# Attention and a two-layer network in one kernel: the first v split ahead of w_out, the last w_out blocks later in the load order, the second scores in one PSUM bank

## The chip, the cores and the metric

The kernel runs on one core of a Trainium2 chip. Measured is the device time of one execution in microseconds; the profile is of one such execution. TensorE (PE, with its weight loads PEld) multiplies, VectorE (DVE) and ScalarE (ACT) work on vectors, SyncE's queue (SP) issues the DMAs. Each engine takes its instructions in the order of the program.

## The reference, cut to what matters

```python
# q, k, v: (2, 6016, 256);  w_in: (256, 2048);  w_out: (2048, 256);  alpha: (2048,)
qn = q / (norm(q, axis=1) + 1e-6)          # norm over the 6016 rows
kn = k / (norm(k, axis=1) + 1e-6)
s  = kn.transpose(0, 2, 1) @ qn / tau      # (2, 256, 256)
a  = softmax(s, axis=-1)                   # sum + 1e-9
x  = (v @ a).reshape(12032, 256)
h  = x @ w_in
g  = maximum(h, 0) + alpha * minimum(h, 0)
out = g @ w_out                            # (12032, 256)
```

## The kernel before, in words

The order of all work is written out by hand (`tc.manual_schedule()`): an engine runs its instructions in the order in which the program names them, and the framework only adds the waits that the data and the buffers ask for.

**Scores.** q and k of a batch come in 25 chunks, `load_kq`, of two blocks of 128 rows (the first and the last two chunks of one). `chunk_pe` (L357) multiplies a chunk into two 128x256 sums S of the batch, 8 matmuls for a chunk of two blocks; `chunk_elem` takes the squares of batch 0. S0 is summed first. Its norms, scores, exponentials and transposes follow, while TensorE goes on with the first chunks of S1 (batch 1). Before, S1 lies in the two banks `o0` and `o1`, which stage two of the items uses afterwards.

**M.** `x @ w_in` is folded: for each of 8 pairs of blocks (NPAIR) of w_in, `m_pe` (L482) multiplies the softmax with w_in, `m_sums` (L493) makes sums of its quarters on ScalarE and VectorE and `m_split` (L510) splits them into a rounded high part and a low part (`split`, L93 to L98). The loop of L708 does this for j = 0 to 7, with a chunk or two of S1 on TensorE beside each.

**Weights.** w_in and w_out come as 64-bit numbers in 8 blocks each. `conv_a` (L218, ScalarE, L189 to L191) and `conv_b` (L227, VectorE, L195 to L202) convert block c: c = 0 to 7 are w_in's, 8 to 15 w_out's. `split_wo` (L242) then splits a w_out block into high (ScalarE, L248) and low (VectorE, L249). In the loop of L708 pass j converts block j + 3 (ScalarE) and j + 2 (VectorE), so w_out's blocks 0 to 2 are begun in it. After the loop the kernel before runs the S1 chunks up to number 19 and splits w_out blocks 0 to 7 in order; the first v split stands behind `split_wo(5)`, and behind ScalarE's conversion of block 7.

**v.** v comes transposed in 24 tiles of 504 or 500 columns, 12 a batch. `v_sums` (VectorE, L287), `v_high` (ScalarE, L306) and `v_low` (VectorE, L312) make seven combinations of a tile's quarters and split them. The raw tile has one buffer, the split tiles have two (`vspl`); each pair of conversions took one of these as scratch.

**Items.** The main loop (L807) goes over 192 items, tile by tile, 8 pairs each. An item's first stage multiplies M with v in seven products of three matmuls (`pe_a` to `pe_d`; L102 to L104). ScalarE copies the first into two banks (`copies`, L543, L544), VectorE adds one product over (`add_p7`, L560, once with n = 0 after `pe_b`, once with n = 1 after `pe_c`), ScalarE and VectorE apply the function (`act_n`, L572; `dve_g`, L581) and split the result (`g_high`, L590; `g_low`, L594). Stage two (`stage2`, L599; L618) runs three items later: 12 matmuls with w_out in two parts of 5 and 7. `pe_c` of an item needs its L560 of n = 0; `pe_d` writes what the L560 of n = 1 reads and waits for it. In items 0 to 2, which have no stage two, six places are filled with the last chunks of S1 (FILL = 5 of them), and `evac` (L368, two VectorE copies, L371) takes S1 out behind the last. `at_item(i, f)` puts side work behind item i's own: the split of the next v tile, batch 1's norms and M.

Four "set" matmuls (L744) stand ahead of item 0; they write the four banks of the first stage once, with the first v split as moving operand.

**Loads.** The list `mix` gives the order of the loads behind S0's: i a w_in block, k an S1 chunk (two DMAs), o a w_out block, v the first v tile. Each kind has its ring of buffers: `raw`, 4 buffers, for i, o and later the transposed q and k; `m`, `gh` and `gl` for the chunks. A load is put in SP's queue at the point of the program where its buffer has come free, and never past another that still waits; in the queue it waits for the last reader of that buffer. The load of the next v tile is issued where `v_low(t, 0)` stands.

Of the kernel before, what the change touches and what calls it, by code (L numbers as in the profile page):

```python
# [8 lines left out]
F32 = mybir.dt.float32  # L9
F32R = mybir.dt.float32r  # L10
U32 = mybir.dt.uint32
# [3 lines left out]
P = 128  # L15
TW = 512
# [1 line left out]
LATE = 3  # L18
TL = 1024
WARM = 8  # L20
FILL = 5


@with_exitstack
def fused_kernel(
# [28 lines left out]
    B, N, C = q.shape  # L54
    DFF = w_in.shape[1]
    DM = w_out.shape[1]
    KC = C // P
# [3 lines left out]
    NPAIR = NF // 2  # L61
# [28 lines left out]
    def f32(ap):  # L90
        return ap.bitcast(F32)
# [15 lines left out]
    class Loads:  # L107


        def __init__(self, rings):  # L110
            self.free = dict(rings)
            self.todo = []
# [39 lines left out]
    big = {}  # L152
# [21 lines left out]
    def convert_a(w, src, c):  # L174

        if c % 2 == 0:
            big["cv"] = vpool.tile([P, 2, 3, 512], U32, tag="vspl", name=f"cv{c}")
        s = big["cv"][:, c % 2]
        d, a, l = s[:, 0], s[:, 1], f32(s[:, 2])
        if w is None:
            w = l
        nc.scalar.activation(f32(d), f32(src[:, :, 1]), AF.Copy, scale=2.0**-112)  # L189
        nc.scalar.activation(l, src[:, :, 0], AF.Copy, scale=2.0**-29, bias=2.0**23)  # L190
        nc.scalar.activation(l.bitcast(U32), l, AF.Copy, bias=-(2.0**23))  # L191
        return d, a, l, w
# [25 lines left out]
    def conv_a(c):  # L218

        if c < NPAIR:  # L220
            src, w = wi_raw.pop(c).rearrange("p k f t -> p (k f) t"), wi[:, c].rearrange("p k f -> p (k f)")
        else:
            src, w = wo_raw.pop(c - NPAIR).rearrange("p f m t -> p (f m) t"), None
        half[c] = convert_a(w, src, c)
        loads.done("raw")

    def conv_b(c):  # L227
        w = convert_b(nc.vector, *half.pop(c))
        if c >= NPAIR:
            wo32[c - NPAIR] = w  # L230
# [11 lines left out]
    def split_wo(i):  # L242

        w = wo32.pop(i).rearrange("p (f m) -> p f m", f=2)
        for fi in range(2):
            f = 2 * i + fi
            s = sgn[:, f : f + 1]
            nc.scalar.activation(wo[:, 0, f], w[:, fi], AF.Copy, scale=s)  # L248
            nc.vector.scalar_tensor_tensor(  # L249
                out=wo[:, 1, f], in0=w[:, fi], scalar=s, in1=f32(wo[:, 0, f]),  # L250
                op0=ALU.mult, op1=ALU.subtract,
            )
# [24 lines left out]
    def v_sums(t, part):  # L277
        h = tiles[t][2] // 2
        x = v_raw[t]
        if part == 0:  # L280
            v_tmp[t] = vtpool.tile([P, 4, HW_], F32, tag="vt", name=f"vt{t}")
        s = v_tmp[t]
        b11, b12 = x[:, 0, :h], x[:, 0, h : 2 * h]
        b21, b22 = x[:, 1, :h], x[:, 1, h : 2 * h]
        sums = ((1, b12, b11), (3, b22, b12), (2, b22, s[:, 1, :h]), (0, b21, s[:, 2, :h]))
        for o, i0, i1 in sums[2 * part : 2 * part + 2]:
            nc.vector.tensor_tensor(out=s[:, o, :h], in0=i0, in1=i1, op=ALU.subtract)  # L287
# [13 lines left out]
    def v_high(t, part):  # L301
        h = tiles[t][2] // 2
        if part == 0:
            v_spl[t] = vpool.tile([P, 2, 7, HW_], F32R, tag="vspl", name=f"vs{t}")
        for sl, x in v_parts(t, part):
            nc.scalar.copy(v_spl[t][:, 0, sl, :h], x)  # L306
# [27 lines left out]


    class Attn:
        def __init__(self, b, S):
            self.b = b
            self.S = S
            self.sums = sm.tile([P, KC], F32, tag="sums", name=f"sums{b}")  # L340
# [16 lines left out]
        def chunk_pe(self, ci):  # L357
            n = chunks[ci][1]
            t = kq_raw.pop((self.b, ci))
            for j in range(n):  # L360
                for cc in range(KC):
                    nc.tensor.matmul(  # L362
                        self.S[cc], t[:, 0, j, cc * P : cc * P + P], t[:, 1, j, :],
                        start=ci == 0 and j == 0, stop=ci == NCH - 1 and j == n - 1,
                    )
            loads.done(kq_ring(self.b, ci))

# [142 lines left out]
    def m_split(at, j):  # L510
        b = at.b
        m = mpool.tile([P, 2, 7, P], F32R, tag="m", name=f"m{b}_{j}")
        split(m[:, 0], m[:, 1], mx.pop((b, j))[:, 0:7], nc.scalar)
        M[b, j] = m
# [116 lines left out]
    with tc.manual_schedule():  # L631
# [18 lines left out]
        for ci in range(NCH):  # L650
            loads.add(kq_ring(0, ci), lambda ci=ci: load_kq(0, ci))
            if ci == 4:
                loads.add("small", load_small)
        mix = "iikikikkikikikikkkkokkokvkokkokkkookkkkoko"
        count = dict.fromkeys("ikov", 0)
        for x in mix:
            j = count[x]
# [24 lines left out]
                a0.chunk_pe(ci - LATE)  # L682
        np_ = ps_r.tile([P, TW], F32, tag="r1", name="np0")
        pb = ps_r.tile([P, TW], F32, tag="r1", name="pb0")
        pt = [ps_q.tile([P, TW], F32, tag="q", name="pt0"), ps_a.tile([P, TW], F32, tag="at", name="pt1")]
        po = [ps_o.tile([P, TW], F32, tag=f"o{cc}", name=f"S1_{cc}") for cc in range(KC)]
        a1 = Attn(1, [x[:, 0:C] for x in po])
        conv_a(0)
        a0.chunk_pe(NCH - 3)
        conv_b(0)  # L690
# [15 lines left out]
        a0.split_eT(1)  # L706
        nxt = 3
        for j in range(NPAIR):  # L708
            conv_a(j + 3)
            conv_b(j + 2)  # L710
            if j < 2:
                a1.chunk_pe(nxt)
                nxt += 1
            m_pe(a0, j, ps_r, f"r{j % 2}")
            a1.chunk_pe(nxt)
            nxt += 1
            m_sums(a0, j)
            if j:
                m_split(a0, j - 1)
        m_split(a0, NPAIR - 1)  # L720
        while nxt < NCH - FILL:
            a1.chunk_pe(nxt)
            nxt += 1
        split_wo(0)
        conv_a(NPAIR + 3)
        for i in range(2, NPAIR):
            conv_b(NPAIR + i)
            split_wo(i - 1)
            if i + 2 < NPAIR:
                conv_a(NPAIR + i + 2)  # L730
            if i == NPAIR - 2:
                for part in range(2):
                    v_sums(0, part)
                for part in range(3):
                    v_high(0, part)
                for part in range(3):
                    v_low(0, part)
        split_wo(NPAIR - 1)

        h = max(w for _, _, w in tiles) // 2  # L740
        assert h == tiles[0][2] // 2
        for f in (0, 1, 0, 1):
            x = ps_r.tile([P, 2, HW_], F32, tag=f"r{f}", name="set")
            nc.tensor.matmul(  # L744
                x[:, :, :h], wo[:, 0, 0, 0:P], v_spl[0][:, 0, 0:2, :h], start=True, stop=True,
                skip_group_check=True,
            )

# [3 lines left out]
        def at_item(i, f, *args):  # L752
            side.setdefault(i, []).append((f, args))


        i = NPAIR + 4
        for p in range(len(pieces)):
# [24 lines left out]
            at_item(i, lambda j=j: (m_pe(a1, j, ps_a, "at"), m_sums(a1, j)))  # L782
            at_item(i + 1, lambda j=j: m_split(a1, j))
        for t in range(1, len(tiles)):
            i = (t - 1) * NPAIR + 1
            at_item(i, v_sums, t, 0)
            at_item(i + 1, v_sums, t, 1)
            at_item(i + 1, v_high, t, 0)
            at_item(i + 2, v_high, t, 1)
            at_item(i + 2, v_low, t, 0)  # L790
            at_item(i + 3, v_high, t, 2)
            at_item(i + 3, v_low, t, 1)
            at_item(i + 4, v_low, t, 2)

        fill = iter(range(NCH - FILL, NCH))

# [73 lines left out]
```

## Time and profile before

| | |
|---|---|
| median of 3 runs | 1137.34 us (1136.93 to 1138.18) |
| profiled execution | 1138.28 us, its span 1136.4 us |
| TensorE busy | 1118.8 us, 98% of the span |
| VectorE busy | 840.9 us, 74% |
| ScalarE busy | 810.7 us, 71% |
| DMA | 71.14 MB, most of it in the first tenth of the span |

Times of single instructions are microseconds from the span's start. In a timeline a row is a run of like instructions: its start, the time from the first start to the last end, the engine, the line, the operation, what it writes and reads, how many, and in brackets the engine's idle time before it with what ended it. Instructions of one engine overlap a little when they follow each other without a wait, so the distance from start to start is shorter than the duration; the ends of matmuls are modelled.

### The profile page before, as it was taken

What the parts mean: (1) busy time and instruction counts of PE and PEld (TensorE: products, weight loads), DVE (VectorE), ACT (ScalarE), POOL (GpSimd) and SP (SyncE); (2) the same over time, 40 slices, a digit from 0 to 9 for tenths busy, and PEclk for the clock granted to TensorE, in tenths of its full rate; (3) what the DMA queues carried; (4) which work ended last, traced back from release to release, by engine and by line L of the source; (5) the groups of instructions that cost most, each with busy time, mean ns of one, the idle gap of its engine ahead of it and who ended that gap; (6) DMA issues with size and microseconds to landing.
All of it is one profiled execution on the core that took longest, in us unless ns stands there. A gap on an engine that the chain in (4) does not pass through costs nothing.

```text
span 1136.4 us, 17786 instructions
## 1 busy us (share of the span) xinstructions
PE 1118.8 (98%) x6884; PEld 1008.8 (89%) x6884; DVE 840.9 (74%) x1562; ACT 810.7 (71%) x1498; POOL 1.7 (0%) x8
## 2 busy tenths in 40 slices
PE   9996999999999999999999999999999999999998
PEld 8885899889999999899999989999999999999997
DVE  6787777777777777877777877777777777777765
ACT  6786677877877776776776766766776776776764
POOL 0000000000000000000000000000000000000000
PEclk9997999999999999999999999999999999999999
DMA  9997002222222110110100101100100100110000
GB/s 338 346 320 272 20 19 59 88 72 75 74 73 73 53 37 1 37 36 2 37 21 17 38 1 37 38 10 28 37 19 19 37 19 19 37 31 8 19 20 18
DMA packets 36019, 71.14 MB, mean 63 GB/s; under 512 B 3680, under 2 KB 17504, under 8 KB 35936
## 3 DMA queue, kind: packets, MB, share of 16 engines
q1 hardware_dynamic: 35936, 70.01, 18.5%
q8 instruction: 54, 0.88, 0.3%
q14 instruction: 29, 0.24, 0.1%
HBM read 57.68 MB, written 12.32 MB: 62 GB/s over the span
## 4 chain that ended last, share of the span: by engine, by line
PE 93%; DVE 3%; DMA 2%; ACT 1%; issue 0%; SPq 0%; POOL 0%; DVEq 0%; ACTq 0%; POOLq 0%
PE o L618 46%; PE r L102 10%; PE r L104 10%; PE r L103 10%; PE S L362 4%; PE q L103 4%; PE q L104 4%; PE q L102 4%; PE pm L491 1%; DMA wo<-w_out_dram 1%; DMA kq<-q_dram 1%; DVE m L98 0%; DMA kq<-k_dram 0%; PE warm L639 0%; DVE cv L199 0%
## 5 line engine op out<-in xcount | busy, mean ns | idle before, releaser
L618 PE MATMUL o<-gh,wo 128*128 128x500 f32 (+1 forms) x1536 | 508.7, 392 | 1.4 <-ACT ob L622 1.4
L581 DVE SCALAR_TENSOR_TENSOR g<-r,sgn,g 128x500 f32<-128x500 f32 (+1 forms) x384 | 282.3, 735 | 106.6 <-ACT g L572 106.6
L618 PEld LDWEIGHTS o<-gh,wo 128*128 128x128 f32 x1536 | 276.4, 188 | 41.3 <-ACT ob L622 1.6
L618 PE MATMUL o<-gl,wo 128*128 128x500 f32 (+1 forms) x768 | 299.3, 390 | 0.0
L572 ACT ACTIVATE g<-r,salpha 128x500 f32<-128x500 f32 (+1 forms) x384 | 262.8, 688 | 22.2 <-PE r L104 1.5
L560 DVE TENSOR_TENSOR r<-r,p 128x250 f32<-128x250 f32 (+1 forms) x384 | 163.7, 426 | 145.0 <-PE r L104 145.0
L102 PE MATMUL r<-vs,m 128*128 128x250 f32 (+1 forms) x960 | 269.1, 280 | 1.0 <-DVE r L560 0.8
L104 PE MATMUL r<-vs,m 128*128 128x250 f32 (+1 forms) x960 | 268.1, 279 | 0.0
L103 PE MATMUL r<-vs,m 128*128 128x250 f32 (+1 forms) x960 | 267.8, 279 | 0.0
L590 ACT CAST gh<-g 128x500 fp32r<-128x500 f32 (+1 forms) x384 | 230.0, 613 | 48.9 <-DVE g L581 45.8
L543 ACT COPY r<-q 128x500 f32<-128x500 f32 (+1 forms) x192 | 108.3, 564 | 201.6 <-PE q L104 201.6
L594 DVE TENSOR_TENSOR gl<-g,gh 128x500 fp32r<-128x500 f32 (+1 forms) x384 | 242.5, 673 | 4.7 <-ACT gh L590 4.7
L102 PEld LDWEIGHTS r<-vs,m 128*128 128x128 f32 x960 | 180.9, 188 | 17.6 <-DVE r L560 1.0
L103 PEld LDWEIGHTS r<-vs,m 128*128 128x128 f32 x960 | 181.5, 189 | 15.3
L104 PEld LDWEIGHTS r<-vs,m 128*128 128x128 f32 x960 | 181.4, 189 | 0.0
L618 PEld LDWEIGHTS o<-gl,wo 128*128 128x128 f32 x768 | 144.1, 188 | 23.6
L103 PE MATMUL q<-vs,m 128*128 128x250 f32 (+1 forms) x384 | 107.5, 280 | 0.4 <-DVE vs L312 0.4
L104 PE MATMUL q<-vs,m 128*128 128x250 f32 (+1 forms) x384 | 107.6, 280 | 0.0
L102 PE MATMUL q<-vs,m 128*128 128x250 f32 (+1 forms) x384 | 107.4, 280 | 0.0
L362 PE MATMUL S<-kq 128*128 128x256 f32 x332 | 76.0, 385 | 0.0
L103 PEld LDWEIGHTS q<-vs,m 128*128 128x128 f32 x384 | 72.6, 189 | 0.7 <-DVE vs L312 0.7
L102 PEld LDWEIGHTS q<-vs,m 128*128 128x128 f32 x384 | 72.6, 189 | 0.3 <-ACT vs L306 0.3
(82 smaller groups left out, 716.2 us busy)
## 6 DMA issues: line engine op xcount, KB each, us to landing
kqT<-kqT_dram SPq DMA_DIRECT2D x20, 512.0 KB, 3.6
kq<-k_dram SPq DMA_DIRECT2D x39, 256.0 KB, 5.5
kq<-q_dram SPq DMA_DIRECT2D x39, 256.0 KB, 5.6
v<-vT_dram SPq DMA_DIRECT2D x16, 500.0 KB, 3.6
outT_dram<-ob SPq DMA_DIRECT2D x32, 250.0 KB, 2.0
wi<-w_in_dram SPq DMA_DIRECT2D x8, 512.0 KB, 5.5
wo<-w_out_dram SPq DMA_DIRECT2D x8, 512.0 KB, 5.7
v<-vT_dram SPq DMA_DIRECT2D x8, 504.0 KB, 3.6
```

Source lines behind the costliest of these rows:

```text
L102: nc.tensor.matmul(out, wh, xh, start=first, stop=False, **s)
L103: nc.tensor.matmul(out, wh, xl, start=False, stop=False, **s)
L104: nc.tensor.matmul(out, wl, xh, start=False, stop=last, **s)
L362: nc.tensor.matmul(self.S[cc], t[:, 0, j, cc * P : cc * P + P], t[:, 1, j, :], start=ci == 0 and j == 0, stop=ci == NCH - 1 and j == n - 1,)
L491: nc.tensor.matmul(o, at.eT[:, d, cs], wi[:, j, d, :], start=first, stop=last)
L543: nc.scalar.copy(r_t[i][0][:, :, :h], x[:, 0:1, :h].broadcast_to([P, 2, h]))
L560: nc.vector.tensor_tensor(out=r[1][:, n, :h], in0=r[0][:, 1, :h], in1=p7_t[i][:, :h], op=ALU.add)
L572: nc.scalar.activation(by_half(g_t[i][:, fi], i), r_t[i][fi][:, :, : half_of(i)], AF.Copy, scale=salpha[:, f : f + 1],)
L581: nc.vector.scalar_tensor_tensor(out=g, in0=r_t[i][fi][:, :, : half_of(i)], scalar=sgn[:, f : f + 1], in1=g, op0=ALU.mult, op1=ALU.max,)
L590: nc.scalar.copy(gs_t[i][0][:, fi, :w], g_t[i][:, fi, :w])
L594: nc.vector.tensor_tensor(out=gs_t[i][1][:, fi, :w], in0=g_t[i][:, fi, :w], in1=f32(gs_t[i][0][:, fi, :w]), op=ALU.subtract,)
L618: nc.tensor.matmul(o, x, y, start=first, stop=last)
```

## The change

- The scratch of the conversions becomes one tile of 7 parts, used in turn; a w_in block uses 2 (its third is the block itself), a w_out block 3. It takes one of the two `vspl` buffers, so the first v split has the other.
- In the load order the first v tile and w_out blocks 0 to 5 come earlier, each block between single S1 chunks; blocks 6 and 7 come behind chunks 18 and 24.
- S1's two sums share the bank `at`; only the first of the two clears it. The second tile of batch 0's transposes goes to `r1`.
- `split_wo(0)` goes into the last pass of the M loop, ahead of `conv_a(10)`; the whole first v split follows the loop at once. `wo_next(i)` (split block i, ScalarE's part of block i + 2, VectorE's of i + 1) runs for 1 and 2 behind it and, as side work, for 3 to 7 in items 0 to 4.
- FILL goes from 5 to 6: chunk 19 becomes the first fill.
- The set matmuls take a block of M in place of one of w_out as weights.
- The v split of tile 1 runs in items 4 to 7 in place of 1 to 5.

```diff
-FILL = 5
+CV = 7
+FILL = 6
...
-        if c % 2 == 0:
-            big["cv"] = vpool.tile([P, 2, 3, 512], U32, tag="vspl", name=f"cv{c}")
-        s = big["cv"][:, c % 2]
-        d, a, l = s[:, 0], s[:, 1], f32(s[:, 2])
+        if c == 0:
+            big["cv"] = vpool.tile([P, CV, 512], U32, tag="vspl", name="cv")
+            big["at"] = 0
+
+        def part():
+            i = big["at"]
+            big["at"] = (i + 1) % CV
+            return big["cv"][:, i]
+
+        d, l = part(), f32(part())
         if w is None:
-            w = l
+            a, w = part(), l
+        else:
+            a = w.bitcast(U32)
...
-                        start=ci == 0 and j == 0, stop=ci == NCH - 1 and j == n - 1,
+                        start=ci == 0 and j == 0 and not (self.shared and cc),
+                        stop=ci == NCH - 1 and j == n - 1, skip_group_check=self.shared,
...
-        mix = "iikikikkikikikikkkkokkokvkokkokkkookkkkoko"
+        mix = "iikikikkikikikik" + "ko" * 2 + "v" + "ko" * 4 + "k" * 5 + "o" + "k" * 6 + "o"
...
-        pt = [ps_q.tile([P, TW], F32, tag="q", name="pt0"), ps_a.tile([P, TW], F32, tag="at", name="pt1")]
-        po = [ps_o.tile([P, TW], F32, tag=f"o{cc}", name=f"S1_{cc}") for cc in range(KC)]
-        a1 = Attn(1, [x[:, 0:C] for x in po])
+        pt = [ps_q.tile([P, TW], F32, tag="q", name="pt0"), ps_r.tile([P, TW], F32, tag="r1", name="pt1")]
+        po = ps_a.tile([P, KC, C], F32, tag="at", name="S1")
+        a1 = Attn(1, [po[:, cc] for cc in range(KC)], shared=True)
...
         for j in range(NPAIR):
+            if j == NPAIR - 1:
+                split_wo(0)
             conv_a(j + 3)
             conv_b(j + 2)
...
         m_split(a0, NPAIR - 1)
+        for part in range(2):
+            v_sums(0, part)
+        for part in range(3):
+            v_high(0, part)
+        for part in range(3):
+            v_low(0, part)
+
+        def wo_next(i):
+
+            split_wo(i)
+            if i + 2 < NPAIR:
+                conv_a(NPAIR + i + 2)
+            if i + 1 < NPAIR:
+                conv_b(NPAIR + i + 1)
+
+        for i in (1, 2):
+            wo_next(i)
         while nxt < NCH - FILL:
             a1.chunk_pe(nxt)
             nxt += 1
-        split_wo(0)
-        conv_a(NPAIR + 3)
-        for i in range(2, NPAIR):
-            conv_b(NPAIR + i)
-            split_wo(i - 1)
-            if i + 2 < NPAIR:
-                conv_a(NPAIR + i + 2)
-            if i == NPAIR - 2:
-                for part in range(2):
-                    v_sums(0, part)
-                for part in range(3):
-                    v_high(0, part)
-                for part in range(3):
-                    v_low(0, part)
-        split_wo(NPAIR - 1)
...
-                x[:, :, :h], wo[:, 0, 0, 0:P], v_spl[0][:, 0, 0:2, :h], start=True, stop=True,
+                x[:, :, :h], M[0, 0][:, 0, 0], v_spl[0][:, 0, 0:2, :h], start=True, stop=True,
...
+        for i in range(3, NPAIR):
+            at_item(i - 3, wo_next, i)
...
-            i = (t - 1) * NPAIR + 1
-            at_item(i, v_sums, t, 0)
-            at_item(i + 1, v_sums, t, 1)
-            at_item(i + 1, v_high, t, 0)
-            at_item(i + 2, v_high, t, 1)
-            at_item(i + 2, v_low, t, 0)
-            at_item(i + 3, v_high, t, 2)
-            at_item(i + 3, v_low, t, 1)
-            at_item(i + 4, v_low, t, 2)
+
+            when = (1, 2, 2, 3, 3, 4, 4, 5) if t > 1 else (4, 4, 5, 5, 6, 6, 7, 7)
+            steps = (
+                (v_sums, 0), (v_sums, 1), (v_high, 0), (v_high, 1),
+                (v_low, 0), (v_high, 2), (v_low, 1), (v_low, 2),
+            )
+            for i, (f, part) in zip(when, steps):
+                at_item((t - 1) * NPAIR + i, f, t, part)
```

## Rows read from the trace of the kernel before

**Rows 1.** The page: part 1, and S's line of part 5 (busy, mean ns).

```profile
PE 1118.8 (98%) x6884; PEld 1008.8 (89%) x6884; DVE 840.9 (74%) x1562; ACT 810.7 (71%) x1498; POOL 1.7 (0%) x8
...
L362 PE MATMUL S<-kq 128*128 128x256 f32 x332 | 76.0, 385 | 0.0
```

**Rows 2.** The list of waits: engine, what, line <- releaser: us, times, longest.

```profile
PE set L744 <- ACT vs L306: 10.0, 1, 10.0
```

**Rows 3.** Timeline of all engines, 78 to 118 us.

```profile
81.61 13.98 PE L362 MATMUL S<-kq 128*128 128x256 f32 x64
...
104.56 0.92 ACT L306 CAST vs<-v 128x252 fp32r<-128x252 f32 x2 [0.56 <-DVE wo L249]
...
105.53 2.05 PE L744 MATMUL set<-vs,wo 128*128 128x504 f32 x4 [9.95 <-ACT vs L306]
...
112.42 0.47 PE L102 MATMUL r<-vs,m 128*128 128x252 f32 x1
```

**Rows 4.** Windows of 10 us: length, busy by engine (instructions), PEclk, DMA share, GB/s.

```profile
100.00:110.00 10.00, 4.12 (x12) 3.21 (x13) 8.76 (x19) 6.90 (x15) 0.00 (x0) 0.50 0.71 243
...
120.00:130.00 10.00, 9.20 (x63) 8.38 (x62) 9.68 (x21) 8.28 (x16) 0.00 (x0) 1.00 0.01 2
```

**Rows 5.** Chain of waits in order of time: start, us, what.

```profile
133.43 1.61 PE o L618 x7
...
138.64 1.61 PE o L618 x7
```

**Rows 6.** Timeline, VectorE at the M loop's end.

```profile
80.48 1.02 DVE L507 TENSOR_TENSOR mx<-mx 128x128 f32<-128x128 f32 x4
...
81.41 1.09 DVE L98 TENSOR_TENSOR m<-mx,m 128x896 fp32r<-128x896 f32 x1
```

**Rows 7.** Timeline, w_out blocks on ScalarE, then on VectorE.

```profile
92.71 0.89 ACT L248 ACTIVATE wo<-cv,sgn 128x256 fp32r<-128x256 f32 x2
...
93.51 0.66 ACT L189 ACTIVATE cv<-wo 128x512 f32<-128x512 f32 x1
...
95.31 0.89 ACT L248 ACTIVATE wo<-cv,sgn 128x256 fp32r<-128x256 f32 x2
...
94.03 0.42 DVE L195 TENSOR_SCALAR cv<-cv 128x512 uint32<-128x512 uint32 x1
...
95.84 0.88 DVE L249 SCALAR_TENSOR_TENSOR wo<-cv,sgn,wo 128x256 fp32r<-128x256 f32 x2
```

**Rows 8.** Timeline, VectorE in items 1 and 2, and TensorE's wait.

```profile
119.41 0.43 DVE L560 TENSOR_TENSOR r<-r,p 128x252 f32<-128x252 f32 x1 [0.57 <-PE r L104]
...
119.75 0.73 DVE L581 SCALAR_TENSOR_TENSOR g<-r,sgn,g 128x504 f32<-128x504 f32 x1
...
120.40 0.74 DVE L287 TENSOR_TENSOR vt<-v 128x252 f32<-128x252 f32 x2
...
121.39 1.27 DVE L594 TENSOR_TENSOR gl<-g,gh 128x504 fp32r<-128x504 f32 x2
...
122.57 0.75 DVE L371 COPY sr<-S 128x256 f32<-128x256 f32 x2
...
123.24 0.73 DVE L581 SCALAR_TENSOR_TENSOR g<-r,sgn,g 128x504 f32<-128x504 f32 x1
...
124.36 0.38 PE L102 MATMUL r<-vs,m 128*128 128x252 f32 x1 [0.80 <-DVE r L560]
```

**Rows 9.** Timeline, ScalarE reading raw blocks.

```profile
63.23 0.67 ACT L190 ACTIVATE cv<-wi 128x512 f32<-128x512 uint32 x1
...
77.04 0.67 ACT L190 ACTIVATE cv<-wo 128x512 f32<-128x512 uint32 x1
```

**Rows 10.** The page, part 6: DMA issues, KB each, us to landing.

```profile
v<-vT_dram SPq DMA_DIRECT2D x8, 504.0 KB, 3.6
```

**Rows 11.** Windows of 2 us.

```profile
64.00:66.00 2.00, 2.00 (x11) 1.77 (x10) 1.93 (x6) 2.00 (x4) 0.00 (x0) 1.00 1.04 384
...
82.00:84.00 2.00, 2.00 (x11) 1.74 (x11) 1.93 (x4) 1.47 (x3) 0.00 (x0) 1.00 0.57 206
```

More of the change, by code (lines that the diff above doesn't have):

```diff
@@ L336, in fused_kernel, with __init__ @@
     class Attn:
-        def __init__(self, b, S):
+        def __init__(self, b, S, shared=False):
+            self.shared = shared
             self.b = b
```

## The prediction

> **What bounds the kernel now.** I read the page first, then the list of waits, then the timeline around the longest of them, then the windows for the clock.
>
> The page: TensorE is busy 98% of the span, VectorE and ScalarE 74% and 71% [rows 1]. So the end is TensorE's own work plus the moments in which it does not run. The waits: one of these is far ahead of all others, 10.0 us of the matrix engine at the "set" matmuls, for ScalarE's L306, the first rounded half of the first v split [rows 2].
>
> The timeline shows why [rows 3]. The matmuls of S1 run without a gap up to about 95.6 us and then there is nothing to do. L306 stands in ScalarE's queue behind the conversion of the last w_out blocks, which itself waits for their loads; v's turn comes at 104.56, TensorE goes on at 105.53. The clock pays too: over 100 to 110 us the granted clock is 0.50, the lower of its two levels [rows 4]. From 105.53 to 112.42 TensorE does 3.4 us worth of work at the full clock (priced below), so some 3.5 us go there. Later there is one 0.80 us wait.
>
> **What TensorE has to do in this stage.** Call chunk 18 the last chunk of S1 that both kernels do ahead of the items. The 64 matmuls from 81.61 on are chunks 12 to 19: 13.98 us less one matmul's 0.39 (its mean, [rows 1]) over 63 steps is 0.216 a step, 1.73 a chunk. Chunk 18 ends at 81.61 + 7 x 1.73 = 93.7.
>
> One item in steady state lasts 138.64 - 133.43 = 5.21 us, a second-stage matmul 1.61/7 = 0.23 [rows 5]. That leaves (5.21 - 12 x 0.23)/21 = 0.117 for each first-stage matmul. Between chunk 18 and the start of item 6 stand chunks 19 to 24 (8.65), 4 set matmuls (0.9), 117 first-stage matmuls (13.65) and 36 of stage two (8.3): 31.5 us. With no gap at all item 6 would start at 125.2. In the kernel before it starts at 138.64 + 1.61 = 140.25 [rows 5]: 15 us are lost, 10.0 waiting, 3.5 by the clock, 0.8 in item 2, the rest in single small starts. From item 6 on both kernels have the same work, TensorE-bound, so the start of item 6 is where I compare them.
>
> **The change, part by part.** *v split first.* Nothing is added: w_out block 0, the v split, then w_out blocks 1 to 7, each with the same instructions. When is v ready? VectorE has no gap here. At 80.48 it starts the sums of M block 6 (0.93), then a subtraction of L98 (1.05) [rows 6]. Then come w_out block 0's low halves (0.80), the conversion of block 1 (1.81, priced below), M block 7's sums 0.93, two L98 2.15: 88.1. The four v sums (1.3, priced below) end at 89.4, the four v subtractions (2.2, priced as L594 by columns) at 91.6; ScalarE's parts fit between. TensorE wants them at 93.7 + 0.9 = 94.6: the 10 us wait goes, and with it the clock's fall. If this cover of 3.0 us were gone, each us late costs one.
>
> *w_out blocks 1 to 7 beside the items.* This takes the place of the old wait. Prices, start to start where the engine had no gap: the split of a block 0.80 on ScalarE (92.71 to 93.51) and the same taken on VectorE (0.88 whole); the rest of a block 1.80 on ScalarE (93.51 to 95.31) and 1.81 on VectorE (94.03 to 95.84) [rows 7]. Item work on VectorE: L560 0.34, L581 0.65, the L594 pair 1.18, the two copies of S1 0.67; two v sums and one L560 take 0.99 together [rows 8].
>
> VectorE's queue from the end of the v split (91.6) to the L560 that item 5's pe_d waits for: 7 splits 5.6, 6 conversions 10.9, 10 L560 3.4, 8 L581 5.2, 3 pairs of L594 3.5, the copies 0.7, the v sums of tile 1, 1.3: 30.6 us. VectorE itself waits some 3.4 us in it: 0.6 for ScalarE's first half of block 2 (94.2 to 94.8), 0.9 for pe_b of item 0 (97.5 to 98.4), 1.35 for item 0's first L572 (behind conversion and copies on ScalarE), 0.55 for pe_b of item 1. So it gets there at 91.6 + 30.6 + 3.4 = 125.6. Behind it TensorE has pe_d 0.35, pe_b 0.70 and 7 matmuls 1.61: item 6 starts at 128.3.
>
> Seen from TensorE it is 128.6: 125.2 without gaps and 3.4 us of waits, which I get by walking the three queues item by item: 0.5 before item 0's pe_b (its copies stand behind w_out block 4's conversion on ScalarE, until 97.5), 0.25 twice in items 2 and 3, 1.7 before pe_d of item 2 (VectorE ends item 1's last L581 at 110.95; split, conversion and copies of S1 bring it to 114.2, L560 ends at 114.65, while TensorE has been ready for pe_d since 112.95), 0.55 and 0.15 in items 4 and 5. A wait of this kind is seen in the kernel before: 0.80 at 124.36, where v sums and the copies stand ahead of an L560 [rows 8].
>
> Bounds: if VectorE's work hides fully, 125.2. If operations cost their whole durations and not their steps (0.43, 0.73, 1.27, 0.75 for the copies, 0.88 for a split, [rows 7, 8]), VectorE's sum grows by 0.9 + 0.65 + 0.3 + 0.1 + 0.55 = 2.5 and item 6 starts at 131. I take 128.5, between the two walks: the steps are from a stretch as dense as the new one.
>
> *Tile 1's v split* goes 3 items later, since its buffer is the scratch that block 7's split sets free. Its last subtraction now ends just before item 8's second matmul wants it; I count 0.2.
>
> *Loads.* The raw ring has 4 buffers, and the SP queue issues in order. So w_out block 1 cannot be issued before ScalarE has read w_in block 5 (63.9), and the later S1 chunks wait behind it; w_out block 5's load goes out at 77.7, when ScalarE has read w_out block 1 [rows 9], and chunks 14 to 17 right behind. A 504 KB load that nothing disturbs lands after 3.6 us [rows 10]; at 384 GB/s [rows 11] 512 KB take 1.36 us, so a first byte comes about 2.2 us after issue. Block 5 lands by 81.5, chunk 14 by 83, wanted at 81.61 + 2 x 1.73 = 85.1; chunk 18 (issued 83.4) by 88, wanted at 92. Nothing is late, with 2 to 4 us in hand. The next v load waits in SP for the first v subtraction, until 90.5, and chunks 19 to 24 are queued behind it: chunk 19 lands at about 95.4, wanted at 95.3, and the copies on ScalarE hold item 0 until 97.5 anyway. Cost nothing.
>
> *S1 in one bank, the transposes in r1, the conversion's scratch, the set weights, one chunk more as fill.* No instruction more or longer. Zero, with less than 0.2 either way, since all of it runs under a busy TensorE.
>
> **Sum.** 140.25 - 128.5 = 11.7 us less, minus 0.2: 11.5. The profiled execution took 1138.28 (span 1136.4, 1.9 around it, which stays), so it would take 1126.8; the median of the runs is 0.94 lower, 1125.8. I predict **1125.8**.
>
> **Rivals.** *A: the conversions hide fully*, 15.0 us gained, 1122.3. For it: VectorE has about 1.5 us free of each 5.2 us item. Against: the stages that are to hide them also have less TensorE work in them (chunks 23 and 24 are half size).
>
> *B: the work costs more than its steps*, or the clock falls in the new gaps. The first gives 140.25 - 131 = 9.2, so 1128.3. The second: the gaps of items 2 to 5 come close together. Over 120 to 130 us, with the 0.80 us wait inside, the granted clock stayed 1.00 [rows 4]; if it fell once, the price is the one of the kernel before, 3.5 us, and the time 1129.3. [...]
>
> *C, the other side: S1's chunks come late.* The place is SP's queue, blocked until 63.9 [rows 9] and then paced by ScalarE. From the first byte at 66 to chunk 18 there are 15 loads of 512 KB, 7.9 MB. At the 206 GB/s of a thin stretch [rows 11] they take 38 us and chunk 18 comes at 104, 12 us late: 1137.3 + 0.5 = 1138 or more, with a clock fall 1141. The point from which it decides is 227 GB/s. Against: the rate is 206 where little was asked for, 384 where the queue was full.
>
> *D: v is not ready either*, because VectorE is further behind at 88 us than the rows say. Up to 3.0 us late costs nothing; each further us costs one. A gain of 4 to 7 would be left: 1132.
>
> **How the numbers follow.** Forecast (1123.5 to 1127.5) 0.53; A 0.12; B 0.20; D 0.06; no change 0.04; C and what is like it 0.05. A measurement of this kernel can tell about 0.2%, 2.3 us, from no change. So faster 0.91, same 0.04, slower 0.05. The range leaves out the far end of D, no change and C: 1122.0 to 1131.
>
> **What would show it.** The set matmuls start at about 94, without a 10 us wait; the clock row of 100 to 110 us is 1.00; ScalarE's L306 for tile 0 comes ahead of w_out block 1's L248; pe_d of item 2 waits 1 to 2 us for L560 behind a conversion; item 6's start is near 128.5. Wrong would be: a gap in S1's matmuls before 93 us (C), the first L102 of item 0 waiting for L312 (D), a clock under 1.00 after 95 us (B).

## The result and the profile after

The changed kernel takes 1127.54 us (median of 5 runs, 1127.29 to 1128.17), the kernel before in the same session 1137.83: a ratio of 0.9907 with a 95% interval of 0.9896 to 0.9918, so 10.6 us faster (9.3 to 11.8). The forecast was 1125.8, with 1122.0 to 1131 as range. The profiled execution took 1127.84 with a span of 1125.9, 10.5 less than before.

Line numbers have moved by some ten lines: L306 is now L315, L362 L373, L491 L503, L560 L572, L618 L630, L744 L760, and so on.

The page answers to [rows 1]: TensorE's busy time fell by 2.6 us, its share went up.

```profile
PE 1116.2 (99%) x6884; PEld 1005.8 (89%) x6884; DVE 839.5 (75%) x1562; ACT 810.5 (72%) x1498; POOL 1.7 (0%) x8
```

TensorE's waits in the list of waits (engine, what, line <- releaser: us, times, longest). The 10.0 us of [rows 2] are gone; in their place stand small ones, two for VectorE's L572 and one for a load of S1. The rows for L630 and "warm" were there before.

```profile
PE r L103 <- DVE r L572: 1.7, 2, 1.4
PE o L630 <- ACT ob L634: 1.4, 1, 1.4
PE S L373 <- DMA kq<-q_dram: 1.1, 1, 1.1
PE warm L651 <- POOL ones L646: 1.0, 1, 1.0
```

The timeline of the stage, which answers to [rows 3]:

```profile
81.30 12.25 PE L373 MATMUL S<-kq 128*128 128x256 f32 x56
...
86.64 0.91 ACT L315 CAST vs<-v 128x252 fp32r<-128x252 f32 x2
...
90.15 1.27 DVE L321 TENSOR_TENSOR vs<-vt,vs 128x504 fp32r<-128x504 f32 x2
90.26 0.38 SPq L279 DMA_DIRECT2D v<-vT_dram  x1
90.37 0.90 ACT L257 ACTIVATE wo<-cv,sgn 128x256 fp32r<-128x256 f32 x2
90.73 0.42 SPq L169 DMA_DIRECT2D kq<-k_dram  x1
...
93.20 1.25 PE L760 MATMUL set<-vs,m 128*128 128x504 f32 x4
...
96.24 1.97 PE L373 MATMUL S<-kq 128*128 128x256 f32 x8 [1.09 <-DMA kq<-q_dram]
...
97.85 0.47 PE L103 MATMUL r<-vs,m 128*128 128x252 f32 x1
```

Chunks 12 to 18 (56 matmuls) run straight into the set matmuls at 93.20. ScalarE has rounded the first part of v at 86.64, four us ahead of w_out block 1 (90.37), and VectorE's last v subtraction begins at 90.15. The load of v tile 1 stands in SP ahead of chunk 19 (90.26 and 90.73), and here TensorE waits 1.09 us.

VectorE ahead of the largest wait, and that wait on TensorE:

```profile
110.87 0.73 DVE L593 SCALAR_TENSOR_TENSOR g<-r,sgn,g 128x504 f32<-128x504 f32 x1
111.52 0.87 DVE L258 SCALAR_TENSOR_TENSOR wo<-cv,sgn,wo 128x256 fp32r<-128x256 f32 x2
112.31 0.42 DVE L204 TENSOR_SCALAR cv<-cv 128x512 uint32<-128x512 uint32 x1
112.76 0.69 DVE L208 SCALAR_TENSOR_TENSOR cv<-cv 128x512 uint32<-128x512 uint32 x1
113.49 0.69 DVE L211 CUSTOM_DVE_ANT_0 cv<-cv 128x1024 uint16<-128x1024 uint16 x1
114.10 0.75 DVE L383 COPY sr<-S 128x256 f32<-128x256 f32 x2
114.76 0.42 DVE L572 TENSOR_TENSOR r<-r,p 128x252 f32<-128x252 f32 x1
...
115.24 0.38 PE L103 MATMUL r<-vs,m 128*128 128x252 f32 x1 [1.41 <-DVE r L572]
```

Windows of 10 us (length, busy by engine, PEclk, DMA share, GB/s) against [rows 4]: the granted clock is 1.00 throughout, though TensorE is busy for only 8.59 of 10 us in the second.

```profile
100.00:110.00 10.00, 9.88 (x65) 8.93 (x65) 8.15 (x17) 7.36 (x16) 0.00 (x0) 1.00 0.64 224
110.00:120.00 10.00, 8.59 (x54) 7.22 (x53) 9.86 (x21) 8.32 (x17) 0.00 (x0) 1.00 0.18 55
120.00:130.00 10.00, 9.76 (x61) 8.23 (x60) 9.06 (x19) 8.22 (x17) 0.00 (x0) 1.00 0.00 0
```

The chain of waits, items 5 and 6, then 7 and 8, against [rows 5]:

```profile
127.66 1.63 PE o L630 x7
132.88 1.61 PE o L630 x7
138.09 1.61 PE o L630 x7
143.47 1.61 PE o L630 x7
```

Item 6 starts at 127.66 + 1.63 = 129.29, against 140.25 before: 10.96 us earlier. Items are 5.21 apart, but 5.38 between 138.09 and 143.47: this is tile 1's v split, which just misses item 8, by 0.17.

### The profile page after: what moved, and what is told of

Read it like the earlier page. It is cut to its first block, busy times and chain, and to the rows that moved or that the text cites. A ratio compares the mean times of both kernels' runs of the same rounds, so it can differ in the third digit from the quotient of the medians.

```text
span 1125.9 us, 17783 instructions
## 1 busy us (share of the span) xinstructions
PE 1116.2 (99%) x6884; PEld 1005.8 (89%) x6884; DVE 839.5 (75%) x1562; ACT 810.5 (72%) x1498; POOL 1.7 (0%) x8
## 4 chain that ended last, share of the span: by engine, by line
PE 94%; DVE 3%; DMA 1%; ACT 1%; issue 0%; SPq 0%; DVEq 0%; ACTq 0%
PE o L630 46%; PE r L103 10%; PE r L105 10%; PE r L104 10%; PE S L373 5%; PE q L105 4%; PE q L104 4%; PE q L103 4%; PE pm L503 2%; DMA kq<-q_dram 1%; DVE m L99 0%; DMA kqs<-q_dram 0%; DVE g L593 0%; DVE wo L258 0%; SPq L169 0%
## 5 line engine op out<-in xcount | busy, mean ns | idle before, releaser
L630 PE MATMUL o<-gh,wo 128*128 128x500 f32 (+1 forms) x1536 | 508.7, 392 | 1.4 <-ACT ob L634 1.4
L593 DVE SCALAR_TENSOR_TENSOR g<-r,sgn,g 128x500 f32<-128x500 f32 (+1 forms) x384 | 282.3, 735 | 105.2 <-ACT g L584 105.2
L630 PEld LDWEIGHTS o<-gh,wo 128*128 128x128 f32 x1536 | 276.4, 188 | 41.3 <-ACT ob L634 1.6
L630 PE MATMUL o<-gl,wo 128*128 128x500 f32 (+1 forms) x768 | 299.3, 390 | 0.0
L572 DVE TENSOR_TENSOR r<-r,p 128x250 f32<-128x250 f32 (+1 forms) x384 | 163.6, 426 | 139.9 <-PE r L105 139.9
L630 PEld LDWEIGHTS o<-gl,wo 128*128 128x128 f32 x768 | 144.1, 188 | 23.6
L373 PE MATMUL S<-kq 128*128 128x256 f32 x332 | 74.8, 379 | 1.1 <-DMA kq<-q_dram 1.1
```

The source lines that it names most:

```text
L373: nc.tensor.matmul(self.S[cc], t[:, 0, j, cc * P : cc * P + P], t[:, 1, j, :], start=ci == 0 and j == 0 and not (self.shared and cc), stop ...
L572: nc.vector.tensor_tensor(out=r[1][:, n, :h], in0=r[0][:, 1, :h], in1=p7_t[i][:, :h], op=ALU.add)
L593: nc.vector.scalar_tensor_tensor(out=g, in0=r_t[i][fi][:, :, : half_of(i)], scalar=sgn[:, f : f + 1], in1=g, op0=ALU.mult, op1=ALU.max,)
L630: nc.tensor.matmul(o, x, y, start=first, stop=last)
```

## The experiments

Executions differ in when the first S0 chunks arrive (TensorE waits 1.1 us for one in e3's, 0.2 in the changed kernel's), which moves all that follows. So beside the times I give the distance from the start of the set matmuls to the start of item 6 (the end of item 5's seven matmuls in the chain), which has the time of this stage and nothing of the start. One thing in it is chance: when chunk 19's load comes. The way from the set matmuls to item 0's pe_b takes 4.65 us in the changed kernel's profiled execution (93.20 to 97.85) and 4.06 to 4.08 in those of e2, e3, e4, e5, e7, e9 and e11. The last column counts from that pe_b on, like with like for the kernels that have w_out blocks beside the items.

| kernel | ratio to before (interval) | us | set | item 6 | distance | from pe_b |
|---|---|---|---|---|---|---|
| before | 1 | 1137.8 to 1138.4 | 105.53 | 140.25 | 34.7 | |
| changed | 0.9907 (0.9896 to 0.9918) | 1127.54 | 93.20 | 129.29 | 36.1 | 31.4 |
| e1, v split late | 1.0001 (0.9992 to 1.0010) | 1138.45 | 103.91 | 140.18 | 36.3 | |
| e2, load order of before | 0.9913 (0.9899 to 0.9926) | 1128.52 | 93.30 | 130.25 | 37.0 | 32.9 |
| e3, v tile 1 loaded later | 0.9902 (0.9889 to 0.9916) | 1127.38 | 94.26 | 129.71 | 35.5 | 31.4 |
| e5, S1 in o0 and o1 | 0.9916 (0.9903 to 0.9930) | 1128.71 | 93.69 | 129.29 | 35.6 | 31.5 |
| e9, copies of S1 four times | 0.9936 (0.9924 to 0.9949) | 1130.72 | 93.74 | 133.17 | 39.4 | 35.4 |
| e4, spread | 0.9894 (0.9881 to 0.9908) | 1125.85 | 93.35 | 127.08 | 33.7 | 29.7 |
| e7, e3 and e4 | 0.9895 (0.9880 to 0.9910) | 1125.67 | 93.28 | 127.02 | 33.7 | 29.7 |
| e11, e4 with S1 in o0 and o1 | 0.9893 (0.9880 to 0.9907) | 1125.68 | 93.27 | 127.05 | 33.8 | 29.7 |
| e6, filler of 44 calls in before | 1.0050 (1.0038 to 1.0063) | 1143.46 | | | | |
| e6b, filler of 22 calls in before | 1.0010 (1.0001 to 1.0019) | 1139.01 | | | | |

**e1: the v split back behind w_out block 5, blocks 3 to 7 ahead of the items again; the rest of the change stays.**

```diff
@@ behind m_split(a0, NPAIR - 1)
-        for part in range(2):
-            v_sums(0, part)
-        for part in range(3):
-            v_high(0, part)
-        for part in range(3):
-            v_low(0, part)
@@ behind the chunks up to 18
+        for i in range(3, NPAIR):
+            wo_next(i)
+            if i == 5:
+                for part in range(2):
+                    v_sums(0, part)
...
-        for i in range(3, NPAIR):
-            at_item(i - 3, wo_next, i)
```

> The changed kernel with the first v split put back behind split_wo(5), and w_out blocks 3 to 7 split ahead of the items again; load order, S1's bank, fills and scratch stay changed. Theory (the place of the v split is the gain): TensorE waits at the set matmuls again, some 8 us (no ScalarE wait for a w_out load now, so up to 2 us less than the 10 us of before), its granted clock falls to half once more, and the time is 1135 to 1138. Rival (the earlier loads of v and w_out are what pays): under 1132, with a wait of 4 us or less.

All of the gain is gone. The wait is 10.22 us, not the 8 that I expected, though no w_out load is waited for now:

```profile
97.11 0.91 ACT L257 ACTIVATE wo<-cv,sgn 128x256 fp32r<-128x256 f32 x2 [0.56 <-DVE cv L211]
...
100.36 0.91 ACT L257 ACTIVATE wo<-cv,sgn 128x256 fp32r<-128x256 f32 x2 [0.57 <-DVE cv L211]
...
103.91 2.05 PE L763 MATMUL set<-vs,m 128*128 128x504 f32 x4 [10.22 <-ACT vs L315]
```

ScalarE and VectorE take turns: a block's high half waits for VectorE's conversion of it, so that blocks come 3.25 us apart (97.11 to 100.36) though neither engine works more than 2.7 us on one. The kernel before does not have this: there the next block's conversion stands on VectorE ahead of a block's low half, and two blocks whose loads are there come 2.60 apart on ScalarE (92.71 and 95.31, [rows 7]). So the new order within a block costs e1 some 2 us (an estimate: 0.65 on each of blocks 3 to 5), part of what the earlier loads save it: v comes at 102.95, 1.6 us before 104.56 [rows 3], and chunk 19, now behind the set matmuls, takes as much again. With the 2 us allowed for, a wait of 8 us would still be left: v behind w_out block 5 brings it back, and most of the gain is the order of v ahead of w_out. e1 moves the w_out blocks back along with v; v first with all blocks ahead of the items was not run. What the load order gives by itself, e1 does not show.

**e2: the load order of before, as far as it still works.**

```diff
-        mix = "iikikikkikikikik" + "ko" * 2 + "v" + "ko" * 4 + "k" * 5 + "o" + "k" * 6 + "o"
+        mix = "iikikikkikikikik" + "kkkokkokvkokko" + "ko" + "kko" + "kkkko" + "ko"
```

> The changed kernel with the load order of before as far as it still works: w_out blocks 2 to 5 and the first v tile later, S1 chunks 8 to 19 earlier (block 4 one chunk ahead of its old place, since its conversion comes earlier now). Theory (the early loads only make room, with 2 to 4 us in hand): 1127 to 1129, all S1 chunks in time, and chunk 19 still waits about 1 us behind the next v load. Rival (loads pay): 1130 or more, with ScalarE waiting for w_out blocks 4 and 5.

Within the theory's band: 0.9 us more distance, 1.4 from pe_b on. The wait is not the one expected (chunk 19 is late by 0.2 and not 1) but at chunk 20, now behind w_out block 5 in the queue:

```profile
99.62 1.97 PE L373 MATMUL S<-kq 128*128 128x256 f32 x8 [1.28 <-DMA kq<-q_dram]
```

The whole order of before could not be tried: the change converts w_out block 4 ahead of S1's chunk 13, so that this block must be loaded earlier. That is what the order is for; beyond that the trace shows some 1 us for it, and the times, whose intervals overlap, can't tell.

**e3: v tile 1's load behind chunk 18.**

```diff
-        if part == 0:
+        if part == 0 and t > 0:
             vloads.done("vraw")
@@ behind the chunks up to 18
+        vloads.done("vraw")
```

> The changed kernel with the load of v tile 1 issued behind chunk 18 in place of inside the first v split, so that S1 chunks 19 to 24 are not queued behind it in SP. Theory (that load in SP's queue makes TensorE wait 1.09 us for chunk 19): the wait goes, 0.4 us then wait for ScalarE's copies, and item 6 starts 0.6 us earlier: 1126.9. Rival (it was the DMA engines' rate, not the queue): the wait stays and the time is 1127.5.

The wait for chunk 19 is gone and one of 0.39 us for ScalarE's copies stands in its place; the distance falls by 0.6, as expected. But the executions of e4, e5, e9 and e11, which load v tile 1 where the changed kernel does, have these 0.6 too, and from pe_b on nothing differs: the gain is one against a single late load, and the time can't tell it.

```profile
98.33 0.39 PE L103 MATMUL r<-vs,m 128*128 128x252 f32 x1 [0.39 <-ACT r L555]
```

**e5: S1 in two banks.**

```diff
-        pt = [ps_q.tile([P, TW], F32, tag="q", name="pt0"), ps_r.tile([P, TW], F32, tag="r1", name="pt1")]
-        po = ps_a.tile([P, KC, C], F32, tag="at", name="S1")
-        a1 = Attn(1, [po[:, cc] for cc in range(KC)], shared=True)
+        pt = [ps_q.tile([P, TW], F32, tag="q", name="pt0"), ps_a.tile([P, TW], F32, tag="at", name="pt1")]
+        po = [ps_o.tile([P, TW], F32, tag=f"o{cc}", name=f"S1_{cc}") for cc in range(KC)]
+        a1 = Attn(1, [x[:, 0:C] for x in po])
```

> The changed kernel with S1 in the two banks o0 and o1 again (and the second transposes in the bank at). Theory of the prediction: one bank or two costs nothing, within 0.2 us, 1127.5. Rival: stage two of item 0 must now wait for the two copies of S1 on VectorE, which end 2.3 us after TensorE is ready for it; of that 1.6 us was waited anyway before pe_d of item 2, so 0.8 to 1.2 us more, 1128.5.

The rival's wait is there, and in the profiled execution the loss it was to bring is not:

```profile
114.43 0.49 PE L630 MATMUL o<-gh,wo 128*128 128x504 f32 x1 [1.89 <-DVE sr L383]
```

Stage two waits 1.89 us for the copies, and the waits for L572 behind it are gone: the same delay of VectorE, met at another matmul. From pe_b on the distance is 31.5, 0.1 more than the changed kernel. The medians differ by 1.2 us, and the clock goes with it: in two of the five executions, the profiled one among them, the mean granted clock was 1.000 and the time 1127.83 and 1127.97; in the other three it was 0.998 and the time 1128.71 to 1129.8. No trace of those three was kept, so where their clock fell is not known; the changed kernel's five executions have 0.999 to 1.000. So the second bank costs about nothing in the executions at 1.000; in the other three the clock was lower.

**e9: the copies of S1 four times.**

```diff
                     if ci == NCH - 1:
                         a1.evac()
+                        for _ in range(3):
+                            for cc in range(KC):
+                                nc.vector.tensor_copy(a1.sr[:, cc], a1.S[cc])
```

> The changed kernel with the two copies of S1 done four times in place of once, 2.0 us more on VectorE behind item 2. Theory (VectorE's queue sets the start of item 6): all of it is seen, the wait before item 2's pe_d grows from 1.6 to 3.5 us and the time by 1.8 to 2.0 us. Rival (the waits in items 2 to 5 are single delays with room behind them): less than 0.7 us more, because VectorE catches up before item 6.

The wait grew by 1.98 us, from 1.41 to 3.39, just what three more pairs of copies at 0.67 [rows 8] add to VectorE, and the granted clock, 1.00 in the changed kernel, fell behind it to 0.82 and 0.84:

```profile
117.11 0.58 PE L103 MATMUL r<-vs,m 128*128 128x252 f32 x1 [3.39 <-DVE r L572]
```

```profile
110.00:120.00 10.00, 6.61 (x33) 5.48 (x32) 9.38 (x22) 7.08 (x15) 0.00 (x0) 0.82 0.17 53
120.00:130.00 10.00, 10.00 (x55) 8.87 (x54) 8.92 (x20) 5.27 (x12) 0.00 (x0) 0.84 0.01 2
```

From pe_b on the distance grows by 3.9 us: 2.0 of queue and the rest, 1.9, of low clock, net of the small waits that it covered. The time grows by 0.29%, 3.3 us, where 1.8 to 2.0 were expected. VectorE's queue does set this stage, and the fall of the clock that rival B names came here with a wait of 3.39 us, where the changed kernel's longest in this stage is 1.41.

**e4 and e7: the work moved to where VectorE has room.**

```diff
-        for i in range(3, NPAIR):
-            at_item(i - 3, wo_next, i)
+        for i, at in zip(range(3, NPAIR), (0, 1, 3, 4, 5)):
+            at_item(at, wo_next, i)
+        at_item(6, a1.evac)
...
-            when = (1, 2, 2, 3, 3, 4, 4, 5) if t > 1 else (4, 4, 5, 5, 6, 6, 7, 7)
+            when = (1, 2, 2, 3, 3, 4, 4, 5) if t > 1 else (5, 5, 6, 6, 6, 7, 7, 7)
...
-                    if ci == NCH - 1:
-                        a1.evac()
```

> The changed kernel with w_out blocks 5, 6 and 7 split behind items 3, 4 and 5 (not 2, 3, 4), the copies of S1 behind item 6 and tile 1's v split in items 5 to 7. Theory (VectorE has more work in items 2 to 4 than TensorE, and the work is movable): the waits of items 2 to 5, 2.4 us together, shrink below 0.5 and the time falls by 1.9 to 2.3 us against the changed kernel. Rival (VectorE is short over the whole stretch): the waits come back in items 4 to 8 and the time is the same within 0.7 us.

> The spread of the run before this together with the later load of v tile 1. Theory: both gains add, 0.6 us more than the spread alone, about 2.7 us less than the changed kernel. Rival: they don't add, because item 0's copies on ScalarE hold TensorE once chunk 19 is in time.

The spread takes 1125.85, 1.7 us under the changed kernel, a little less than the 1.9 to 2.3 expected (span 1123.8 against 1125.9; distance 2.4 less, 1.8 of it from pe_b on). What the list of waits still has of this stage:

```profile
PE r L103 <- DVE r L572: 0.2, 1, 0.2
PE r L103 <- ACT r L555: 0.2, 1, 0.2
PE S L373 <- DMA kq<-q_dram: 0.2, 1, 0.2
```

So VectorE is not short over the stretch; items 2 to 4 had too much. (From start to start 1.9 us of waits are left; the next section tells why the list shows less.) That e4 is faster than the changed kernel rests on the trace and the spans; the two intervals against before overlap. In e7 the gains don't add, its rival holds: with chunk 19 in time the copies on ScalarE come next, and in e4 chunk 19 was late by only 0.19, so that the copies held it already.

```profile
97.36 0.39 PE L103 MATMUL r<-vs,m 128*128 128x252 f32 x1 [0.40 <-ACT r L555]
```

**e11: the spread with S1 in two banks**, its copies behind the last chunk again (e5's edit on e4, without `at_item(6, a1.evac)`).

> The spread of the w_out blocks with S1 in the two banks o0 and o1, so that its copies stand behind the last chunk again and item 0's stage two waits for them. Theory (the bank is worth nothing where VectorE is not behind: its copies end at 111.2, stage two can start at 112.0): the same as the spread alone, 1125.9 within 0.4. Rival (one bank is worth a wait of its own): 1126.6 or more, with a wait of the first stage-two matmul for the copies.

The same time, the same distance (33.8), no wait of stage two. So where VectorE is not behind, the shared bank has no value of its own: it only moves the point where a late VectorE is felt.

**e6 and e6b: TensorE kept busy in the old wait**, to price the low clock of the kernel before; e6b has 22 calls in place of 44.

```diff
+        keep = ps_a.tile([P, TW], F32, tag="at", name="keep")
+        for _ in range(44):
+            nc.tensor.matmul(keep[:, 0:C], wi[:, 0, 0, 0:P], wi[:, 0, 1, :], start=True, stop=True)
```

> The kernel before, with 44 matmuls of 256 columns without use (about 9.5 us, into the free bank at) put on TensorE in the 10 us in which it waits for the first v split. Theory of the prediction (the low clock costs 3.5 us there): the granted clock of 100 to 110 us stays 1.00 and the time falls by 3 to 3.5 us. Rival (in that stretch TensorE also waits for the last v subtraction until 108.1 and for ScalarE's copies until 111.3, so the clock hides behind them): the clock stays up and the time falls by 1.1 us, since item 0's pe_b starts at 111.3 in place of 112.4.

> The kernel before with 22 calls without use in TensorE's 10 us wait: the run with 44 showed that an fp32 call is two matmuls in the trace (88 records, 19.2 us), so it ran 9 us past v. Now the filler takes 9.5 us and ends about when v is ready. Theory of the prediction (the clock costs 3.5 us): 1134.3 to 1134.8. Rival (VectorE's last v subtraction and ScalarE's copies of item 0, behind the split of the last w_out block, hold TensorE anyway): 1136.5 to 1137.

e6 was my error: one fp32 call is two matmuls in the trace, and the filler ran 19.16 us. It still shows what the stretch takes with all operands ready and a granted clock of 1.00 (110 to 120 us): set matmuls at 114.14, item 0's pe_b at 117.49, so 3.35 us, which is the 3.4 of the prediction. e6b is not clean either: the loads of w_out blocks 4 and 6 landed 1.2 us later than in the run of before (ScalarE goes on with them at 92.09 and 100.02, there at 90.89 and 98.76), so v came later, and the time, 1.2 us above before, is neither the theory's nor the rival's. Inside it the answer can be read:

```profile
105.89 0.92 ACT L306 CAST vs<-v 128x252 fp32r<-128x252 f32 x2 [0.55 <-DVE wo L249]
...
106.86 1.18 PE L748 MATMUL set<-vs,wo 128*128 128x504 f32 x4 [1.48 <-ACT vs L306]
...
108.52 0.38 PE L102 MATMUL q<-vs,m 128*128 128x252 f32 x1 [0.48 <-ACT vs L306]
...
109.47 0.47 PE L103 MATMUL q<-vs,m 128*128 128x252 f32 x1 [0.57 <-DVE vs L312]
...
112.06 0.57 ACT L543 COPY r<-q 128x504 f32<-128x504 f32 x1
...
113.34 0.47 PE L102 MATMUL r<-vs,m 128*128 128x252 f32 x1
```

The set matmuls now run at a granted clock of 1.00 (106 to 108 us), the four in 1.18 us where before took 2.05 [rows 3], and then TensorE waits for ScalarE, for VectorE's subtraction and (with the clock down again, 0.50 in 110 to 112) for the copies at 112.06. From v's first part (L306) to pe_b are 113.34 - 105.89 = 7.45 us, before 112.42 - 104.56 = 7.86 [rows 3]: the clock is worth 0.4 us so far. Had it stayed up, chunk 20 would have ended before the copies and pe_b come at some 112.7 (an estimate: the first copy's end), another 0.7. The kernel before shows the same without a filler:

```profile
108.14 0.58 PE L103 MATMUL q<-vs,m 128*128 128x252 f32 x1 [0.35 <-DVE vs L312]
...
110.73 0.57 ACT L543 COPY r<-q 128x504 f32<-128x504 f32 x1
```

pe_b needs this copy, which stands behind the split of a w_out block on ScalarE and ends at 111.30; pe_b came at 112.42 [rows 3]. So the low clock can have cost 1.1 us there at most. The rival's 1.1 fits; 3.5 does not. The executions of e6b point the same way: three of the eleven have a mean granted clock of 0.999 or 1.000 and took 1137.9 to 1138.4, the other eight have 0.997 or 0.998 and took 1138.8 to 1140.3.

## Why the prediction was right, and where not

*The 10 us wait goes.* Right, and e1 shows that the place of the v split against the w_out blocks does it. v was priced to be ready at 91.6; the last subtraction began at 90.15 and ended at 91.4.

*VectorE's queue takes its place.* Right. The walk had L572 of item 2 end at 114.65 after split, conversion and copies, and TensorE wait 1.7; it ended at 115.18, and TensorE waited 1.41 by the list, 1.7 from start to start. Waits of 0.55 and 0.15 later were 0.24 and none in the list, 0.5 and 0.2 from start to start. e9 shows that added VectorE work comes through whole, e4 that moved work does not. Pricing by steps and not by whole durations held: on VectorE L593 at 110.87 is followed by L258 at 111.52, 0.65 later.

*Chunk 19 costs nothing.* Wrong by 1.1 us at the matmul in the profiled execution, 0.8 beyond the 0.5 put down for the copies there. The load was put at 95.4 and came at 96.1, 4.9 us after its last issue. In e4, with the same loads in the same order, TensorE has it at 95.49 and waits 0.19:

```profile
95.49 1.97 PE L373 MATMUL S<-kq 128*128 128x256 f32 x8 [0.19 <-DMA kq<-q_dram]
...
97.41 0.39 PE L103 MATMUL r<-vs,m 128*128 128x252 f32 x1
```

So the price was sound and the margin was not: a chunk put 0.1 us behind its time has nothing in hand when a load comes late. Why it came late is open. The DMA engines moved 45 GB/s in 90 to 92, just before; in e4, e5 and e11 the load landed 4.0 to 4.1 us after its last issue.

*The clock is worth 3.5 us in the kernel before.* Wrong in its share, not in the sum. The 3.5 us between 105.53 and 112.42 were mostly waits for the last v subtraction and for ScalarE's copies, which the low clock covered; the end of the copies and e6b leave about 1 us for the clock. In windows of half a us that clock was 0.50 from 99.0 to 112.0, 0.77 and 0.58 in the windows on either side, and 1.00 in the rest of the span. Both parts went with the change, so the total was not hurt.

*TensorE's own work is 31.5 us.* Right: counted from start to start it is 31.4. The distances are 0.4 longer by the way they are read: the first fp32r matmul (on rounded operands) behind a chunk's fp32 ones starts some 0.2 early (1.53 us behind the chunk's start in the rows below, not 1.73) and the one behind it as much late (0.31, not 0.117), so the set row starts before chunk 18 has had its last step; and the end of item 5's last matmul is modelled 0.17 past the next start. What is left above that is waits, and more than the list has:

```profile
98.75 1.89 PE L373 MATMUL S<-kq 128*128 128x256 f32 x8
100.28 0.47 PE L103 MATMUL r<-vs,m 128*128 128x252 f32 x1
100.59 0.28 PE L104 MATMUL r<-vs,m 128*128 128x252 f32 x1
...
107.71 1.02 PE L373 MATMUL S<-kq 128*128 128x256 f32 x4
108.85 0.39 PE L103 MATMUL r<-vs,m 128*128 128x252 f32 x1
109.08 0.28 PE L104 MATMUL r<-vs,m 128*128 128x252 f32 x1
```

A full chunk and one small matmul take 1.84 us (98.75 to 100.59), just the 1.73 + 0.117 of the prediction. Chunk 23, of 4 matmuls, and one small matmul take 1.37 (107.71 to 109.08) where the price is 0.98: the difference is a wait for L572, which ended at 108.80. It is not in the list, because matmul rows last longer than the way to the next start (chunk 23's 1.02 us, its four steps of 0.216 only 0.86) and cover it.

Counted in this way, waits took 4.3 us where 3.4 were forecast: 1.3 before item 0's pe_b (0.5 forecast), 0.6 behind chunks 23 and 24 (0.5), 1.7 before pe_d of item 2 (1.7), 0.7 in items 4 and 5 (0.7). So the one term of the walk that missed is the first, by chunk 19. The kernel before loses 14.9 us in the same way up to item 6; 10.6 less is the gain that was measured. Against the 0.9 us of waits too few, chunk 18 ended 0.3 earlier (the row of S1 starts at 81.30, not 81.61): item 6 at 129.29, forecast 128.5.

*Tile 1's v split*, 0.2: measured 0.17. *S1's bank* was put at nothing: e11 agrees, and so does e5's trace, but in three of e5's five executions the mean clock was 0.998 and the time some 1 to 2 us longer.

*Rivals.* A does not hold as it stands (4.3 us of waits); in e4 1.9 us of waits are left, and its time is 3.5 above A's. B: the clock did not fall in the changed kernel, after waits of up to 1.41 us close together: its row of 110 to 120 is 1.00 with 1.4 us idle. It fell in e9, to 0.82 in 110 to 120 with a wait of 3.39 us, and in e6b behind several short waits, 1.00 in 106 to 108 and 0.50 in 110 to 112 behind waits of 1.48, 0.48 and 0.57 us; three executions of e5 have a mean of 0.998. C: no S1 chunk before 19 was late. D: v's last part was ready at 91.4 and item 0's second matmul wanted it at 94.40, 3.0 us in hand as forecast.

The median lies 1.7 above the forecast. The profiled execution lies 1.0 above it (1127.84 against 1126.8), 0.8 of it by item 6; the rest is that the forecast took the median to lie below the profiled execution as far as in the three runs of before (0.94), and it lies 0.3 below.

## What to carry to other kernels

When an engine with spare time on average waits once for a long while, look for what stands ahead of the awaited instruction in another engine's queue, and move that past it, to where both engines are busy. Then count the moved work on the receiving engine stage by stage: here three items with less TensorE work than usual took some 3 us back, and shifting a few operations by one item got 1.7 of it again. Count TensorE's time from start to start: a list of waits can leave out what the ends of its rows cover. A time at the low clock is not a price of the clock until one has seen what else would have waited. And a wait in one profiled execution is a finding only when another execution has it too.

## What the runs showed of the hardware that was not expected

- One fp32 matmul call of 256 columns is two matmuls in the trace, 0.216 us each (44 calls, 88 records, 19.16 us); an fp32r call of 504 columns is one (the set, 4 calls and 4 records), of 0.23 (1.61 / 7, [rows 5]).
- Two engines that alternate on one chain of blocks gave one block per 3.25 us, with 2.7 us of work on the busier one (e1).
- Behind chunks 20, 21 and 22 of the changed kernel the first fp32r matmul starts 0.2 us early and the next as much late. Chunk 20: 98.75 to 100.28 is 1.53 us, where 8 steps of 0.216 are 1.73, and 100.28 to 100.59 is 0.31 in place of 0.117. In sum nothing is lost.
- The granted clock stayed at 1.00 in the changed kernel through a wait of 1.41 us. It fell behind one of 3.39 us (e9, 0.82 in 110 to 120), behind three of 1.48, 0.48 and 0.57 us (e6b, 0.50 in 110 to 112), and, with a wait of 1.89 us in its trace, e5 had a mean of 0.998 in three executions of five and 1.000 in two.
